# Two attentions in one launch: A's softmax reductions cut into smaller pieces in more steps, and scores ahead of maxima in the first step of the late groups

## The chip, the core and the metric

The kernel runs on one core of a Trainium2 chip. A core has a matrix engine (TensorE, PE), a vector engine (DVE), a scalar engine (ACT), a general engine (POOL) and a queue that issues DMAs (SyncE, SP). Each runs its own list of instructions in order; they meet only where one waits for another. Times are microseconds of device time, the lower the better; the time of a kernel is the median of several runs. Before the change it is 1596.72 us (three runs, 1595.77 to 1596.78).

## The reference

Two attentions with 32 heads of 18 columns over 2048 positions. A looks at 8 positions back, two apart; B at all positions. Their outputs stand side by side.

```python
def _A_ref(x, wqkv, wo):
    ...
    W, dil = 8, 2
    idx = pos[:, None] - off[None, :]
    mask = idx >= 0
    ...
    logits = jnp.einsum("bhsd,bhswd->bhsw", q, kg) * scale
    logits = jnp.where(mask[None, None, :, :], logits, -1e9)
    attn = _softmax(logits, axis=-1)
    o = jnp.einsum("bhsw,bhswd->bhsd", attn, vg)
    return (lambda x, *d: x.transpose(*d))(o, 0, 2, 1, 3).reshape(B, S, D) @ wo

def _B_ref(x, wqkv, wo):
    ...
    scores = jnp.einsum("bhqd,bhkd->bhqk", q, k) * scale
    p = _softmax(scores, axis=-1)
    o = jnp.einsum("bhqk,bhkd->bhqd", p, v)
    return (lambda x, *d: x.transpose(*d))(o, 0, 2, 1, 3).reshape(B, S, D) @ wo
a = _A_ref(A_x, A_wqkv, A_wo)
b = _B_ref(B_x, B_wqkv, B_wo)
return jnp.concatenate([a, b], axis=-1)
```

## The kernel before

The projections of both attentions come first, up to about 420 us. Then the kernel goes through 512 steps written out by hand. A step is (g, b, kt): a group g of 4 heads of B (8 groups), a block b of 512 queries (4 blocks), a piece kt of 128 keys (16 pieces). So n = step // 16 counts the pairs (g, b) that the diff calls groups behind 22, and kt = step % 16.

In a usual step the engines do this. PE makes four score matrices of 128 x 512 (`score`, line 271) and the products for the maxima of a later block (`take`, line 160): two of 512 columns, and two halves of 256 columns that share a bank (`parts_of_maximum`). Then it multiplies the exponentials of the step before with v into `po` (`weigh`, line 744, sixteen instructions that show as x8 or x16). ACT takes the exponential of the four scores (line 279). DVE reduces the three banks of maxima (`reduce`, line 168). A bank of maxima is free again once DVE has reduced it, and there are three such banks; a bank of scores is free once ACT has read it. DVE has a few other things beside them: the last reduction of a block's maxima (line 178, `m`), its transpose (line 185, `mt`), a reciprocal of B's denominators (line 788) and a copy of `po` (line 759).

What else is due in a step stands in an agenda (`plan`, `later`); `due()` issues it behind the step's own work, so on DVE a piece that is due in step s stands behind that step's three reductions and ahead of those of step s + 1.

A's attention is done beside B's steps, in eight tiles j of 256 positions (`local(j)`). Tile j begins at step AT[j] = 10, 67, 123, 178, 233, 288, 343, 398. Its parts, counted from there: `match` (steps 5 to 25, POOL) makes products of q and k, and ends with the addition that makes the logits `lg`, 128 x 8 x 64 (line 932); `most` (32 and 33, DVE, line 943) takes the maxima over the window of 8, 32 columns in a step; `lower` (33, POOL, line 949) subtracts them; `exponents` (35, ACT, line 952); `total` (36, DVE, line 943) sums over the window, 64 columns at once, or 32 in each of steps 36 and 37 for tiles 0, 2 and 5; `inverses` (38 and 39, DVE, line 959); `share` (39, POOL, line 962) multiplies the exponentials with the inverses; `weighted` (9 parts from step 39 on, POOL, lines 968 to 971) multiplies with v; `upper` and `rest` split the result (60 and 61) and `put` stores it (64 and 66). `SOON` = (3, 0, 0, 0, 1, 1, 1, 0) has these parts begin so many steps sooner (`weighted`, `upper`, `rest` and `put` are put back again by its remainder by 3). The next tile's `match` stands behind them on POOL.

`MADE` lists four steps for each tile. In the step behind each, A's sums are made: that step and the next are then done together as a pair (`together`), with the matrix products of A's output projection between the scores. A pair takes longer than two usual steps.

In the first step of a block (kt = 0) the order on PE is a choice, `ahead`: where it is true, the step's first score stands in front of the first half of a maximum, else behind it. It is true for n < 6, and for n from 24 on except in steps of `MADE`.

Of the kernel before, what the change touches and what calls it, by code (L numbers as in the profile page):

```python
# [11 lines left out]
ALU = mybir.AluOpType  # L12
# [17 lines left out]
SUB = AB // 4  # L30
# [14 lines left out]
MADE = ((96, 101, 112, 128), (144, 160, 176, 192), (208, 212, 224, 240), (256, 266, 272, 288),  # L45
        (307, 320, 336, 352), (368, 376, 384, 400), (417, 432, 440, 448), (474, 476, 478, 480))
# [4 lines left out]
def ap(t, *dims):  # L51

    return bass.AP(tensor=t.tensor, offset=t.offset, ap=[list(t.ap[0])] + [list(d) for d in dims])


def rows(t, *dims):

    return bass.AP(tensor=t.tensor, offset=t.offset, ap=[list(d) for d in dims])
# [3 lines left out]
def two_attentions(ctx: ExitStack, tc, xa, wa, woa, xb, wb, wob, out):  # L62
# [19 lines left out]
    def bank(kind=None):  # L82
        r = rings[kind or ring]
        r.append(r.pop(0))
        return p_bank.tile([128, 512], F32, name=f"bank{r[-1]}")
# [22 lines left out]
    step = 0  # L108
# [8 lines left out]
    def due():  # L117
        for f in agenda.pop(step, []):
            f()
# [89 lines left out]
    def settle():  # L209
        while owing:  # L210
            owing.popleft()()
# [171 lines left out]
    with (tc.tile_pool(name="x", bufs=1, side="right") as xp,  # L383
# [103 lines left out]
        if True:  # L487
# [47 lines left out]
            ahead = deque()  # L535
# [147 lines left out]
            for k in range(2, 14):  # L683
                n = 46 if k == 2 else 36 + 4 * k
# [7 lines left out]
            def leave_a(c, b, n, ps):  # L692
                o = xp.tile([128, 512], F32, name="ohi", bufs=4)
                nc.scalar.activation(o[:n], ps, AF.Copy)  # L694
                load(da[128 * c : 128 * c + n, HALO + 512 * b : HALO + 512 * b + 512], o[:n])
# [23 lines left out]
            for c, b in order:  # L719
                n = min(128, 3 * D - 128 * c)  # L720
                work_list.append(((b % 2, ws[c][0], xas[b][0], slice(0, n), every),
                                  lambda ps, n=n: ps[:n], lambda ps, c=c, b=b, n=n: leave_a(c, b, n, ps)))
# [12 lines left out]
        step = 0  # L735
# [166 lines left out]
    def local(j):  # L902
# [13 lines left out]
        def window(t, c):  # L916

            return ap(t[:, 2 * c, HALO:], (HALO + SUB, 2), (-DIL, W), (1, SUB))

        def wide():  # L920
            return work.tile([128, 2, W, SUB], F32, name="pr", bufs=2)
# [12 lines left out]
                    for w in range(1, W):  # L934
                        nc.gpsimd.memset(lg[:32, w, : DIL * w], MASKED)

        def over_window(op, name, n, parts=2):

            if n == 0:
                st[name] = work.tile([128, SUB], F32, name=name, bufs=1)  # L940
            some = SUB // parts
            cols = slice(some * n, some * n + some)
            nc.vector.tensor_reduce(st[name][:, cols], st["lg"][:, :, cols].rearrange("p w n -> p n w"), axis=AX.X, op=op)  # L943

        def most(n):
            over_window(ALU.max, "am", n)

        def lower():
            nc.gpsimd.tensor_sub(st["lg"], st["lg"], ap(st["am"], (0, W), (1, SUB)))
# [2 lines left out]
            nc.scalar.activation(st["lg"], st["lg"], AF.Exp, scale=SCALE)  # L952

        def total(n):
            over_window(ALU.add, "as", n, len(sums[0]))

        def inverses(n):
            half = st["as"][:, SUB // 2 * n : SUB // 2 * n + SUB // 2]
# [5 lines left out]
        def weighted(c):  # L964
            if c == 0:
                st["o"] = work.tile([128, DH, SUB], F32, name="ao", bufs=1)
            at = wide()
            nc.gpsimd.tensor_mul(at, ap(st["lg"], (0, 2), (SUB, W), (1, SUB)), window(st["v"], c))  # L968
            nc.gpsimd.tensor_add(at[:, :, :4], at[:, :, :4], at[:, :, 4:])  # L969
            nc.gpsimd.tensor_add(at[:, :, :2], at[:, :, :2], at[:, :, 2:4])  # L970
            nc.gpsimd.tensor_add(st["o"][:, 2 * c : 2 * c + 2], at[:, :, 0], at[:, :, 1])
# [10 lines left out]
        def put(i):  # L982
            load(rows(dao[j, i, 0, 0], (DH * SUB, 128), (1, DH * SUB)),
                 ap(st["parts"][i].bitcast(F32), (1, DH * SUB)))
# [24 lines left out]
        def sums_of_a(h, n, alone=True):  # L1009
# [7 lines left out]
            if not alone:  # L1017
# [4 lines left out]


        soon = SOON[j]
        sums = ((36, 37) if j in (0, 2, 5) else (36,), (38, 39))
        late = soon % 3
        pieces = [(33, lower), (35, exponents), (39, share), (60 + late, upper), (61 + late, rest), (64 + late, lambda: put(0)), (66 + late, lambda: put(1))]

        pieces[:0] = [(at, lambda f=f, n=n: f(n)) for f, ats in ((most, (32, 33)), (total, sums[0]),
                                                                (inverses, sums[1])) for n, at in enumerate(ats)]  # L1030
        for c in range(DH // 2):
            pieces.append((39 + 5 * c // 2 + late, lambda c=c: weighted(c)))
        pieces = [(at - soon, f) for at, f in pieces]
        pieces += [(5 + 5 * c // 2, lambda c=c: match(c)) for c in range(DH // 2)]

# [60 lines left out]
    sums = {}  # L1096
# [141 lines left out]
    rest = NG * NB * PIECES * 2 - early  # L1238

    total = early + rest  # L1240

    def together(both, y):

        at = [(*divmod(s // NT, NB), s % NT) for s in (step, step + 1)]
        es = [[None] * 4 for _ in range(2)]
        ps = bank("scores")[:, : y.shape[1]]
        held = rings["scores"].pop()
        exps = deque()

        def one(i, h):  # L1250
            f = score(*at[i], h, put_off=True)
            exps.append(lambda: es[i].__setitem__(h, f()))

        def others(r):
            return [f for i in range(2) for h in (r, r + 2)
                    for f in (lambda i=i, h=h: one(i, h), lambda: maximum(r)())[:: 1 - 2 * r]]

        def piece(r, k):
            a, b = both[r][k]
            return nc.tensor.matmul(ps, a, b, start=r == k == 0, stop=r == 1 and k == len(both[1]) - 1)  # L1260

        def in_turn(*lanes):

            for _, f in sorted(((at + every * k, f) for fs, at, every in lanes for k, f in enumerate(fs)), key=lambda p: p[0]):
                f()
                while len(exps) > 1:
                    exps.popleft()()

        last = []
        in_turn(([lambda k=k: last.append(piece(0, k)) for k in range(len(both[0]))], 0, 133), (others(1), 1, 235))  # L1270
        between = nc.scalar.nop()
        sync(between, last[-1])
        upper = others(0)
        if leaving:
            upper[2] = lambda f=upper[2], copy=leaving.pop(): (f(), exps.popleft()(), copy())
        in_turn(([lambda k=k: sync(piece(1, k), between) if k == 0 else piece(1, k) for k in range(len(both[1]))], 240, 133),
                (upper, 0, 235))
        while exps:
            exps.popleft()()
        nc.scalar.activation(y, ps, AF.Copy)  # L1280
        rings["scores"].append(held)
        rings["scores"].append(rings["scores"].pop(0))
        return [(*at[i], es[i]) for i in range(2)]
# [4 lines left out]
    while step < ALL:  # L1288
        n, kt = divmod(step, NT)
        g, b = divmod(n, NB)  # L1290
        es = [None] * 4

        if inside and inside[0] in for_two and kt and len(ready) == 1 and total - sum(given) >= 8 and step + 4 < ALL:
            new = together(*inside.pop(0)(False))
            assert not leaving
            due()
            step += 1
            weigh(*ready, new[0])
            ready[:] = new[1:]
            due()  # L1300
            step += 1
            continue

        while leaving:
            leaving.pop()()

        whole = total - sum(given) > 1
        parts = (bool(begun) or total - sum(given) > 3) and step not in copied

        ps = bank() if inside and whole else None  # L1310


        ahead = kt == 0 and (n < 6 or n >= 24) and step not in sum(MADE, ())
        part = [parts_of_maximum()] if parts and not ahead else []
        for h in (0, 2, 1, 3):

            if inside and h == 3:
                inside.pop(0)()
            es[h] = score(g, b, kt, h, between=(lambda: part.append(parts_of_maximum())) if parts and ahead and h == 0 else None)
            if h == 0 and whole:  # L1320
                maximum(1, ps)()
            if h == 1 and parts:
                part[0]()
            if h == 3 and whole:
                maximum(0)()
        if sum(given) == total and not begun:
            settle()
        for fs in (behind_scores, outside):
            while fs:
                fs.pop(0)()  # L1330

        paired = paired or kt % 2 == 0 and sum(given) == total and not begun
        for _ in range(1 if paired and step < ALL - 2 else len(waiting)):
            if waiting:
                waiting.pop(0)()
        if ready and (kt % 2 == 0 or not paired):
            weigh(ready.pop(0))
        ready.append((g, b, kt, es))
        if paired and kt % 2:
            weigh(*ready)  # L1340
            ready.clear()
        due()

        if len(waiting) > (0 if not paired else 2 if kt % 2 else len(waiting)):
            waiting.pop(0)()
        step += 1
# [24 lines left out]
```

## Time and profile before

| | |
|---|---|
| median of 3 runs | 1596.72 us (1595.77 to 1596.78) |
| the profiled execution | 1597.76 us, of which its span is 1596.0 us |
| granted TensorE clock | 0.999 |
| DVE's idle time in front of line 168, of it until PE's line 160 is done | 121.6 us, 91.1 us |
| POOL's idle time in front of line 962, waiting for the inverses of line 959 | 63.9 us, 6 times |
| POOL's idle time in front of line 949, waiting for the maxima of line 943 | 41.3 us, 8 times |

In a line of the timeline stand the start, the duration, the engine, the line of the kernel, the operation, what it writes and reads with the shapes, and how many alike follow each other; idle time of 150 ns or more in front of it and what ended it stand in brackets. A line of the table of groups has the number of instructions, then their busy time in all, the mean of one in ns, and the idle time in front of them. The starts of the line with `po` (744) on PE are a clock of the steps: there is one in each.

### The profile page before, as it was taken

The page shows a single profiled execution, that of the slowest core. Times are in us where ns is not written, and L with a number is a line of the kernel's source. Part 1 is how long each engine was busy: PE and PEld are TensorE (multiplying, and loading weights), DVE is VectorE, ACT ScalarE, POOL GpSimd, SP SyncE. Part 2 cuts the span into 40 slices and gives each one's busy share as a digit, 9 for nine tenths or more (in the row PEclk, how much of TensorE's full clock was granted, in tenths as well). Part 3 has the DMA queues.
Part 4 walks back from the last instruction along what each step waited for, and adds up shares of the span by engine and source line. Part 5 has one row for each costly group of instructions (what it writes and reads, how often), then busy time and mean ns, then how long its engine had stood idle before and what let it go on. Part 6 is the DMA issues. An engine that isn't in the chain of part 4 may idle for free.

```text
span 1596.0 us, 34951 instructions
## 1 busy us (share of the span) xinstructions
PE 1583.2 (99%) x13276; PEld 969.1 (61%) x13276; DVE 1367.7 (86%) x2294; ACT 1216.6 (76%) x2438; POOL 964.6 (60%) x798
## 2 busy tenths in 40 slices
PE   9999999999999999999999999999999999999998
PEld 7999889999644445444445445445444444545676
DVE  5199899999999999999989999999999999998622
ACT  6423441211599999999999999999999999998655
POOL 2405742211166996896797897797798699791000
PEclk9999999999999999999999999999999999999999
DMA  8937954622312262245326324522721332154311
GB/s 254 232 124 201 255 178 124 164 90 81 74 34 71 64 143 63 70 118 123 74 67 138 90 79 114 123 67 54 148 89 50 90 94 56 51 166 139 129 60 63
DMA packets 188024, 175.65 MB, mean 110 GB/s; under 512 B 119416, under 2 KB 133240, under 8 KB 186128
## 3 DMA queue, kind: packets, MB, share of 16 engines
q1 hardware_dynamic: 182992, 161.88, 37.0%
q0 software_dynamic: 4032, 10.63, 3.2%
q8 instruction: 104, 1.70, 0.5%
q10 hardware_dynamic: 832, 0.92, 0.2%
q14 instruction: 64, 0.52, 0.1%
HBM read 98.77 MB, written 73.47 MB: 108 GB/s over the span
## 4 chain that ended last, share of the span: by engine, by line
PE 92%; DVE 5%; DMA 1%; ACT 1%; POOL 1%; issue 0%; SPq 0%; POOLq 0%; DVEq 0%; ACTq 0%
PE po L744 29%; PE bank L271 18%; PE bank L160 17%; PE bank L366 15%; PE bank L303 5%; PE bank L1260 4%; PE bank L1133 4%; DVE mx L168 4%; POOL xlo L414 1%; ACT e L279 0%; DMA dqk<-olo 0%; DVE am L943 0%; DMA first<-xb 0%; DMA more<-xa 0%; DMA dqk<-ohi 0%
## 5 line engine op out<-in xcount | busy, mean ns | idle before, releaser
L168 DVE TENSOR_REDUCE mx<-bank 128x2 f32<-128x512 f32 x2048 | 1279.7, 684 | 121.6 <-PE bank L160 91.1
L279 ACT ACTIVATE e<-bank 128x512 f32<-128x512 f32 x2048 | 1048.3, 605 | 61.2 <-PE bank L271 55.3
L160 PE MATMUL bank<-ks,qs 54*128 54x512 f32 (+1 forms) x2466 | 789.0, 381 | 4.2 <-DVE mx L168 3.4
L160 PEld LDWEIGHTS bank<-ks,qs 54*128 54x128 f32 x2466 | 404.1, 184 | 390.2 <-DVE mx L168 343.8
L271 PE MATMUL bank<-qs,ks 56*128 56x512 f32 x2048 | 592.2, 425 | 0.1
L744 PE MATMUL po<-e,v 128*19 128x512 f32 x4096 | 531.3, 598 | 0.0
L271 PEld LDWEIGHTS bank<-qs,ks 56*128 56x128 f32 x2048 | 308.3, 184 | 25.5 <-ACT e L279 18.8
L925 POOL TENSOR_TENSOR pr<-aq,akv 128x1024 f32<-128x1024 f32 x72 | 158.4, 2201 | 15.9 <-PE po L744 13.1
L968 POOL TENSOR_TENSOR pr<-lg,akv 128x1024 f32<-128x1024 f32 x72 | 158.3, 2199 | 0.5
L744 PEld LDWEIGHTS po<-e,v 128*19 128x19 f32 x4096 | 73.8, 97 | 138.2 <-issue 132.8
L929 POOL TENSOR_TENSOR pr<-pr 128x1024 f32<-128x1024 f32 x64 | 152.5, 2383 | 5.0
L694 ACT ACTIVATE ohi<-bank 128x512 f32<-128x512 f32 (+1 forms) x56 | 30.4, 595 | 148.9 <-issue 114.0
L366 PE MATMUL bank<-xhi,ahi 64*128 64x512 f32 (+1 forms) x448 | 115.4, 387 | 0.0
L366 PE MATMUL bank<-xhi,alo 64*128 64x512 f32 (+1 forms) x448 | 111.3, 387 | 0.0
L366 PE MATMUL bank<-xlo,ahi 64*128 64x512 f32 (+1 forms) x448 | 108.3, 388 | 0.1
L1260 PE MATMUL bank<-wohi,at 64*128 64x288 f32 x480 | 104.1, 305 | 0.0
L969 POOL TENSOR_TENSOR pr<-pr 128x512 f32<-128x512 f32 x72 | 92.5, 1285 | 5.6
L1260 PEld LDWEIGHTS bank<-wohi,at 64*128 64x128 f32 x480 | 74.9, 184 | 27.6 <-ACT e L279 23.8
L414 POOL TENSOR_TENSOR alo<-raw,ahi 128x512 fp32r<-128x512 f32 (+1 forms) x14 | 17.6, 1254 | 121.1 <-ACT ahi L413 96.3
L506 POOL TENSOR_TENSOR olo<-olo,ohi 128x512 fp32r<-128x512 f32 x36 | 46.1, 1294 | 65.7 <-ACT ohi L505 55.6
L1260 PE MATMUL bank<-wolo,at 64*128 64x288 f32 x240 | 70.2, 293 | 0.0
L366 PEld LDWEIGHTS bank<-xhi,ahi 64*128 64x128 f32 (+1 forms) x448 | 65.0, 182 | 2.6
(200 smaller groups left out, 1797.3 us busy)
## 6 DMA issues: line engine op xcount, KB each, us to landing
do<-n SPq DMA_DIRECT2D x30, 512.0 KB
da<-ohi SPq DMA_DIRECT2D x52, 256.0 KB
akv<-da SPq DMA_DIRECT2D x64, 175.5 KB
out<-y SPq DMA_DIRECT2D x32, 288.0 KB
qs<-dqk SPq DMA_DIRECT2D x30, 288.0 KB
ks<-dqk SPq DMA_DIRECT2D x30, 288.0 KB
at<-dao SPq DMA_DIRECT2D x60, 128.0 KB
rec<-drec SPq DMA_DIRECT2D x29, 256.0 KB
```

Source lines behind the costliest of these rows:

```text
L160: return nc.tensor.matmul(ps if part is None else ps[:, 256 * r : 256 * r + 256], qs[at, b, p, 128 * t : 128 * t + 128], ks[at, p, 512 * k ...
L168: nc.vector.tensor_reduce(at, ps.rearrange("q (s n) -> q s n", s=2), axis=AX.X, op=ALU.max)
L271: nc.tensor.matmul(ps, ks[at, p, 128 * kt : 128 * kt + 128], qs[at, b, p], start=True, stop=True)
L279: nc.scalar.activation(e, ps, AF.Exp, scale=SCALE)
L303: nc.tensor.matmul(ps, a, b, start=c == i == 0, stop=c == 4 and i == 1)
L366: nc.tensor.matmul(ps, a, b, start=start, stop=stop)
L744: nc.tensor.matmul(po[32 * i : 32 * i + 19], vs[g][:, kt, 19 * i : 19 * i + 19], es[i], start=kt == 0, stop=kt == NT - 1)
L925: nc.gpsimd.tensor_mul(pr, ap(st["q"][:, 2 * c], (SUB, 2), (0, W), (1, SUB)), window(st["k"], c))
L929: nc.gpsimd.tensor_add(st["pr"], st["pr"], pr)
L968: nc.gpsimd.tensor_mul(at, ap(st["lg"], (0, 2), (SUB, W), (1, SUB)), window(st["v"], c))
L969: nc.gpsimd.tensor_add(at[:, :, :4], at[:, :, :4], at[:, :, 4:])
L1260: return nc.tensor.matmul(ps, a, b, start=r == k == 0, stop=r == 1 and k == len(both[1]) - 1)
```

## The change

`most` goes from two pieces of 32 columns in steps 32 and 33 to four pieces of 16 in steps 30 to 33; for tiles 3, 4 and 5 to pieces of 24, 20 and 20 in steps 31 to 33. `total` goes to four pieces of 16 in steps 36 to 39 for tiles 0, 2 and 5, and to pieces of 32, 16 and 16 in steps 36 to 38 for the others. `inverses` go from steps 38 and 39 to 39 and 40 (40 and 41 for tiles 0, 2 and 5), `share` from 39 to 40 (41), and no part of `weighted` is issued ahead of it. `lower` and `exponents` stay. `ahead` is now true for n < 6 and n >= 23 whether or not the step is in `MADE`.

```diff
-        def over_window(op, name, n, parts=2):
-            if n == 0:
+        def over_window(op, name, a, z):
+            if a == 0:
                 st[name] = work.tile([128, SUB], F32, name=name, bufs=1)
-            some = SUB // parts
-            cols = slice(some * n, some * n + some)
+            cols = slice(a, z)
             nc.vector.tensor_reduce(st[name][:, cols], st["lg"][:, :, cols].rearrange("p w n -> p n w"), axis=AX.X, op=op)
...
-            over_window(ALU.max, "am", n)
+            over_window(ALU.max, "am", *highest[n])
...
-            over_window(ALU.add, "as", n, len(sums[0]))
+            over_window(ALU.add, "as", *summed[n])
...
-        sums = ((36, 37) if j in (0, 2, 5) else (36,), (38, 39))
+        alone = j in (0, 2, 5)
+        summed = [(16 * n, 16 * n + 16) for n in range(4)] if alone else [(0, 32), (32, 48), (48, 64)]
+        highest = [(0, 24), (24, 44), (44, 64)] if j in (3, 4, 5) else [(16 * n, 16 * n + 16) for n in range(4)]
...
-        pieces = [(33, lower), (35, exponents), (39, share), ...
+        pieces = [(33, lower), (35, exponents), (40 + alone, share), ...
-        pieces[:0] = [(at, lambda f=f, n=n: f(n)) for f, ats in ((most, (32, 33)), (total, sums[0]),
-                                                                (inverses, sums[1])) for n, at in enumerate(ats)]
+        pieces[:0] = [(at, lambda f=f, n=n: f(n)) for f, ats in ((most, range(34 - len(highest), 34)),
+                                                                (total, range(36, 36 + len(summed))),
+                                                                (inverses, (39 + alone, 40 + alone))) for n, at in enumerate(ats)]
         for c in range(DH // 2):
-            pieces.append((39 + 5 * c // 2 + late, lambda c=c: weighted(c)))
+            pieces.append((max(39 + 5 * c // 2 + late, 40 + alone), lambda c=c: weighted(c)))
...
-        ahead = kt == 0 and (n < 6 or n >= 24) and step not in sum(MADE, ())
+        ahead = kt == 0 and (n < 6 or n >= 23)
```

In the built program ACT's and SP's instructions stand in the same order as before. On PE the order differs in five places, the steps 368, 384, 400, 432 and 448, where the first score and the first half of a maximum change places. DVE has 29 instructions more: 29 reductions for the maxima instead of 16, and 27 for the sums instead of 11. On POOL the order differs around four of the eight `share`: what was due in the steps that `share` has moved past now stands in front of it (a split of A's weights at tile 0, the split of a block's maxima, lines 103 and 104, at tile 4, one subtraction of line 793 at tile 5, and small ones at tile 7).

More of the change, by code (lines that the diff above doesn't have):

```diff
@@ L1024, in local @@
         soon = SOON[j]
-        sums = ((36, 37) if j in (0, 2, 5) else (36,), (38, 39))
+        alone = j in (0, 2, 5)
+        summed = [(16 * n, 16 * n + 16) for n in range(4)] if alone else [(0, 32), (32, 48), (48, 64)]
+        highest = [(0, 24), (24, 44), (44, 64)] if j in (3, 4, 5) else [(16 * n, 16 * n + 16) for n in range(4)]
         late = soon % 3
-        pieces = [(33, lower), (35, exponents), (39, share), (60 + late, upper), (61 + late, rest), (64 + late, lambda: put(0)), (66 + late, lambda: put(1))]
-        pieces[:0] = [(at, lambda f=f, n=n: f(n)) for f, ats in ((most, (32, 33)), (total, sums[0]),
-                                                                (inverses, sums[1])) for n, at in enumerate(ats)]
+        pieces = [(33, lower), (35, exponents), (40 + alone, share), (60 + late, upper), (61 + late, rest), (64 + late, lambda: put(0)), (66 + late, lambda: put(1))]
+        pieces[:0] = [(at, lambda f=f, n=n: f(n)) for f, ats in ((most, range(34 - len(highest), 34)),
+                                                                (total, range(36, 36 + len(summed))),
+                                                                (inverses, (39 + alone, 40 + alone))) for n, at in enumerate(ats)]
         for c in range(DH // 2):
-            pieces.append((39 + 5 * c // 2 + late, lambda c=c: weighted(c)))
+            pieces.append((max(39 + 5 * c // 2 + late, 40 + alone), lambda c=c: weighted(c)))
         pieces = [(at - soon, f) for at, f in pieces]
```

## The prediction

> **What bounds the kernel now.** I read the head of the page first, then the table of DVE's groups with shapes kept apart, then the timeline around A's reductions, and last POOL's part of it.
>
> ```profile
> span 1596.0 us, 34951 instructions
> PE 1583.2 (99%) x13276; PEld 969.1 (61%) x13276; DVE 1367.7 (86%) x2294; ACT 1216.6 (76%) x2438; POOL 964.6 (60%) x798
> PE 92%; DVE 5%; DMA 1%; ACT 1%; POOL 1%; issue 0%; SPq 0%; POOLq 0%; DVEq 0%; ACTq 0%
> ```
>
> The chain runs through PE, and the 5% of DVE in it are places where PE had to wait for a bank of maxima. The steps show how close DVE is to setting the pace. The starts of line 744 are the clock; the am rows are today's maxima of tile 0.
>
> ```profile
> 499.68 1.05 PE L744 MATMUL po<-e,v 128*19 128x512 f32 x8
> 501.08 0.61 DVE L943 TENSOR_REDUCE am<-lg 128x32 f32<-128x256 f32 x1
> 501.70 1.05 PE L744 MATMUL po<-e,v 128*19 128x512 f32 x8
> 503.40 0.60 DVE L943 TENSOR_REDUCE am<-lg 128x32 f32<-128x256 f32 x1
> 503.97 1.05 PE L744 MATMUL po<-e,v 128*19 128x512 f32 x8
> 506.30 1.06 PE L744 MATMUL po<-e,v 128*19 128x512 f32 x8
> ...
> 515.20 1.05 PE L744 MATMUL po<-e,v 128*19 128x512 f32 x8
> 516.63 0.34 DVE L959 RECIPROCAL as<-as 128x32 f32<-128x32 f32 x1
> 517.26 1.05 PE L744 MATMUL po<-e,v 128*19 128x512 f32 x8
> ```
>
> A step takes 2.02 us (501.70 - 499.68). Behind a maximum of 32 columns the next one takes 2.27, then 2.33: 0.25 and 0.31 lost, 0.28 in the mean above some 2.03. The step that follows a reciprocal of 0.34 us takes 2.06, so that is hidden but for 0.03. DVE can thus hide a little over 0.3 us in a step; what goes beyond is paid by the whole kernel.
>
> **The pieces.** These are the rows for DVE's work in question.
>
> ```profile
> L168 DVE TENSOR_REDUCE mx<-bank 128x2 f32<-128x512 f32 x2048 | 1279.7, 684 | 121.6 <-PE bank L160 91.1 <-PE bank L1260 3.7 <-PE bank L366 0.9
> L943 DVE TENSOR_REDUCE am<-lg 128x32 f32<-128x256 f32 x16 | 9.7, 605 | 0.0
> L178 DVE TENSOR_REDUCE m<-mx 128x16 f32<-128x128 f32 x32 | 8.9, 277 | 0.0
> L185 DVE STREAM_TRANSPOSE mt<-m 128x32 f32<-128x32 f32 x32 | 6.3, 198 | 0.0
> L959 DVE RECIPROCAL as<-as 128x32 f32<-128x32 f32 x16 | 5.4, 341 | 0.0
> L943 DVE TENSOR_REDUCE as<-lg 128x64 f32<-128x512 f32 x5 | 5.3, 1064 | 1.9 <-ACT lg L952 1.9
> ```
>
> No row has 16 columns. The line through 605 (32) and 1064 (64) rises 14.3 ns a column from 146 ns, which gives 375 ns for 16, 433 for 20, 490 for 24. Below it lies 277 (line 178 reads as many elements, 128), above it 605 (half the work at the price of the whole). I take 375: two rows of the same operation make the line, and it is nearer to the row with as many elements. At 375 a piece is just above the hidden 341: I charge 0.04 for 16 columns, 0.10 for 20, 0.16 for 24, 0.28 for 32.
>
> Maxima today: 16 x 0.28 = 4.5, less one that stands in the tail of a pair (tile 3, below): 4.2. After: twenty pieces of 16, two of them in a tail, 18 x 0.04 = 0.7; tiles 4 and 5 2 x (0.16 + 0.10 + 0.10) = 0.7; tile 3's last piece and three of 16 fall into steps that also hold an m (0.28), an mt (0.20) or a reciprocal of B's, an estimated 0.9 together, since nothing is left there to hide them. That is 2.3, **1.9 won**.
>
> Sums: tiles 0, 2 and 5 have six of 32 columns, 1.7 today, and twelve of 16 after, with two reciprocals more to the crowd, 0.7: 1.0 won. The other five have one of 64 columns today, in four of them in the tail of a pair, where DVE stands idle anyway. After, the 32 columns stay there, but two pieces of 16 and the reciprocals go into usual steps, and m or mt is in some of these too: 0.2 in each tile by the same prices, **1.0 lost**. Together 0.
>
> **The first step of a block.** What the exchange of score and maximum is worth shows at step 368, against step 416, where the score stands in front already.
>
> ```profile
> 1212.90 1.05 PE L744 MATMUL po<-e,v 128*19 128x512 f32 x8
> 1214.26 0.18 PEld L271 LDWEIGHTS bank<-qs,ks 56*128 56x128 f32 x1 [0.19 <-issue]
> 1215.27 1.05 PE L744 MATMUL po<-e,v 128*19 128x512 f32 x8
> ...
> 1319.86 1.05 PE L744 MATMUL po<-e,v 128*19 128x512 f32 x8
> 1322.02 1.05 PE L744 MATMUL po<-e,v 128*19 128x512 f32 x8
> ```
>
> Step 368 takes 2.37: the first score of a block waits for the loads of its maxima, one after another, and behind a maximum that itself waits for DVE these waits aren't done early. Step 416 takes 2.16. In the built program the score has all eight of these waits at steps 368, 400, 432 and 448, 0.2 won in each; at 384 it has two, and there 2.16 replaces a usual 2.02, 0.14 lost. That is 0.7 won, but 368 and 384 to 400 lie ahead of maxima that will wait for POOL (next part), which eats what is won before them: **0.4**.
>
> **What is moved: `share`, and with it all of POOL.** The inverses stand one step later (two in tiles 0, 2, 5), so `share` does. I asked what POOL does from a tile's `share` to the next tile's logits.
>
> ```profile
> 766.44:866.97 100.53, 100.46 (x824) 47.83 (x822) 92.41 (x153) 97.45 (x193) 96.87 (x70) 1.00 0.41 96
> ```
>
> The columns are the stretch and its length, then PE, PEld, DVE, ACT and POOL: POOL is busy 96.87 of 100.53 us with 70 instructions, 3.66 over 69 gaps, 53 ns each, which is only the distance of two instructions. No row of its timeline in this stretch has an idle bracket, except at `share` itself. POOL is full from each `share` to the next logits, so these come later by what `share` is late. Today the first maximum finds them ready:
>
> ```profile
> 766.44 1.29 POOL L962 TENSOR_TENSOR lg<-lg,as 128x512 f32<-128x512 f32 x1 [12.69 <-DVE as L959]
> 865.69 1.28 POOL L932 TENSOR_TENSOR lg<-pr 128x512 f32<-128x512 f32 x1
> 869.38 0.62 DVE L943 TENSOR_REDUCE am<-lg 128x32 f32<-128x256 f32 x1
> 983.56 1.28 POOL L932 TENSOR_TENSOR lg<-pr 128x512 f32<-128x512 f32 x1
> 988.80 0.60 DVE L943 TENSOR_REDUCE am<-lg 128x32 f32<-128x256 f32 x1
> 1105.44 1.29 POOL L932 TENSOR_TENSOR lg<-pr 128x512 f32<-128x512 f32 x1
> 1109.23 0.60 DVE L943 TENSOR_REDUCE am<-lg 128x32 f32<-128x256 f32 x1
> 1224.16 1.29 POOL L932 TENSOR_TENSOR lg<-pr 128x512 f32<-128x512 f32 x1
> 1230.82 0.60 DVE L943 TENSOR_REDUCE am<-lg 128x32 f32<-128x256 f32 x1
> 1348.28 1.28 POOL L932 TENSOR_TENSOR lg<-pr 128x512 f32<-128x512 f32 x1
> 1353.84 0.61 DVE L943 TENSOR_REDUCE am<-lg 128x32 f32<-128x256 f32 x1
> ```
>
> From the end of the logits to the first maximum these are 2.41, 3.96, 2.50, 5.37 and 4.28 us for tiles 3 to 7. The change takes from it on both sides: the first maximum comes sooner by one step (2.04) in tiles 4 and 5 and two (4.07) in 6 and 7, and the logits come later. By how much follows from the tile before, less the work that `share` now lets past itself, which POOL does while it stands idle anyway:
>
> ```profile
> L793 POOL TENSOR_TENSOR n<-o,n 128x512 fp32r<-128x512 f32 x28 | 36.0, 1284 | 1.3
> L104 POOL TENSOR_TENSOR mt<-mt,mh 128x32 fp32r<-128x32 f32 x32 | 8.1, 252 | 2.6
> L103 POOL CAST mh<-mt 128x32 fp32r<-128x32 f32 x32 | 6.7, 210 | 97.9 <-DVE mt L185 97.9
> ```
>
> Tile 4: 2.04 later, 2.04 + 2.04 - 3.96 = 0.1 us of waiting. Tile 5: 2.04 - 0.46 (lines 103, 104) = 1.58; 2.04 + 1.58 - 2.50 = 1.1. Tile 6: 4.07 - 1.28 (line 793) = 2.79; 4.07 + 2.79 - 5.37 = 1.5. Tile 7: 4.07 + 2.04 - 4.28 = 1.8.
>
> Tile 3 needs more rows, as tile 2's inverses stand in the tail of a pair today, and tile 3's first maxima in another.
>
> ```profile
> 771.11 1.89 DVE L168 TENSOR_REDUCE mx<-bank 128x2 f32<-128x512 f32 x3 [0.18 <-PE bank L160]
> ...
> 870.72 1.89 DVE L168 TENSOR_REDUCE mx<-bank 128x2 f32<-128x512 f32 x3 [0.71 <-PE bank L160]
> ```
>
> Step 164 ends on DVE at 770.93 (771.11 - 0.18); the last inverse then ends 0.34 later and `share` can start at some 771.4, 5.0 behind today's 766.44. The logits end at 866.97 + 5.0 = 871.9. Two pieces (24 and 20 columns) that are due in the pair then take 0.8, so DVE is free at 872.7 instead of 870.72, where the next reduction starts today behind 0.71 of idle time: 2.0. The work of tiles 1 and 2 I leave at no wait.
>
> A wait of DVE is paid in full: behind the first maximum stand the three reductions of the next step, PE waits for the banks that they free, and behind PE's waiting product stand the scores that feed ACT. In all 2.0 + 0.1 + 1.1 + 1.5 + 1.8 = **6.5 lost**. `weighted`, `upper` and `rest` are later with `share`, and so SP's stores of the result, with loads queued behind them. I cost that at nothing: tile 2 stores at step 189 and its first sums are made in step 209, 20 steps or some 41 us later; without that cover a pair would wait for its load.
>
> **The sum**: -1.9 + 0 - 0.4 + 6.5 = +4.2. The profiled execution (1597.76, span 1596.0) goes to 1602.0. It lies 1.04 above the median of the runs, 1596.72, which goes to **1600.9**.
>
> **The rivals.** (a) The logits aren't late: POOL makes up the time, because its spans are rough, or its instructions are shorter when DVE's stand elsewhere. For it speaks that no maximum waits today; against it the full stretch above. From the point where DVE's wait is zero in all tiles, only the gains are left: -1.9 - 0.7 = -2.6, 1594.1, not slower. 14%. (b) Half of the lateness is made up, in part by the 0.7 us that are idle at a pair's tail and the 0.2 in each step: +4.2 - 3.2, 1597.7. 15%. (c) The pieces cost nothing at all and nothing waits: -4.2 - 1.7 - 0.7 = -6.6, 1590.1; the reciprocal's row speaks for it, the crowd of m and mt against it. 7%. (d) Each of the 29 added instructions pays its fixed 146 ns on the path and nothing is won by spreading: +4.2 - 0.7 = +3.5, 1600.2, without a wait for logits. The reciprocal that is hidden speaks against it. 6%. [...]
>
> My own case has 58%.
>
> **How the numbers follow.** The time is that of my case, 1600.9. Its own range is 1598.5 to 1604: each wait may be off by 0.5. Above that lies the dearer piece: at 605 ns the 42 pieces of 16 columns would lose 10 us more (0.24 each), which the rows 605 and 1064 all but exclude, so the range goes only to 1604.5. At 277 ns they would all be hidden and win 1.7. Downwards it takes in (b) and most of (a), to 1594.5. About 0.2% (3.2 us) is what a measurement of this kernel can tell from no change. Slower by more than that: four fifths of my case and half of (d), and a little of (b), 54%. Faster: (c) and a third of (a), 12%. The rest 34%.
>
> **What would show it.** Idle time of DVE in front of line 943 (942 after) that ends with POOL's logits, 1 to 2.5 us in tiles 3, 5, 6 and 7 and none in tiles 0 to 2; POOL full from `share` to logits as today; pieces of 16 columns at 0.375 us and steps of 2.05 to 2.1 around those that don't wait; steps 368, 400, 432 and 448 at 2.16. It is wrong if the maxima wait for nothing, or if DVE's waits don't lengthen the steps.

## The result, and the profile after

| | before | changed |
|---|---|---|
| median of 6 runs each, us | 1596.75 (1595.42 to 1598.99) | 1602.62 (1602.05 to 1603.84) |
| the profiled execution, us | 1597.76 | 1602.72 |
| ratio of the medians | | 1.0037 (95%: 1.0024 to 1.005) |

The kernel is 5.87 us slower (1602.62 - 1596.75), where the prediction has 1600.9, 4.2 slower. The head of the page of the changed kernel comes first.

```profile
span 1600.9 us, 34982 instructions
PE 1582.5 (99%) x13276; PEld 960.2 (60%) x13276; DVE 1367.2 (85%) x2323; ACT 1217.0 (76%) x2438; POOL 965.8 (60%) x798
PE 75%; POOL 14%; DVE 4%; DMA 3%; issue 2%; ACT 1%; SPq 1%; POOLq 0%; DVEq 0%
```

The busy times have hardly moved: DVE has 29 instructions more and 0.5 us less to do, POOL 1.2 us more. What has moved is the chain: POOL had 1% of it and has 14%. The chain is followed backwards and runs along POOL from a tile's logits to its `share` and on, so it says where something waits for POOL, and not that 14% of the time was lost there. The view of the waits gives the size. Its columns are the sum in us, the number and the longest.

```profile
DVE am L942 <- POOL lg L932: 7.5, 4, 2.5
PE bank L160 <- DVE mx L168: 8.2, 8, 2.0
```

The first row has no counterpart before: the maxima never waited for the logits. The second reads so in the kernel before:

```profile
PE bank L160 <- DVE mx L168: 3.4, 15, 0.4
```

There were 15 pieces of at most 0.4 us; now there are single pieces of 2.0. DVE waits for POOL, and PE, which gets no bank back in the meantime, for DVE. The timeline shows the four places and, in its first line, the late `share` of tile 2.

```profile
769.22 1.28 POOL L961 TENSOR_TENSOR lg<-lg,as 128x512 f32<-128x512 f32 x1 [17.42 <-DVE as L958]
...
868.46 1.28 POOL L932 TENSOR_TENSOR lg<-pr 128x512 f32<-128x512 f32 x1
869.78 0.81 DVE L942 TENSOR_REDUCE am<-lg 128x24 f32<-128x192 f32 x2 [2.47 <-POOL lg L932]
...
1107.34 1.29 POOL L932 TENSOR_TENSOR lg<-pr 128x512 f32<-128x512 f32 x1
1108.66 0.49 DVE L942 TENSOR_REDUCE am<-lg 128x24 f32<-128x192 f32 x1 [1.27 <-POOL lg L932]
...
1228.13 1.28 POOL L932 TENSOR_TENSOR lg<-pr 128x512 f32<-128x512 f32 x1
1229.45 0.37 DVE L942 TENSOR_REDUCE am<-lg 128x16 f32<-128x128 f32 x1 [1.79 <-POOL lg L932]
...
1354.09 1.28 POOL L932 TENSOR_TENSOR lg<-pr 128x512 f32<-128x512 f32 x1
1355.40 0.37 DVE L942 TENSOR_REDUCE am<-lg 128x16 f32<-128x128 f32 x1 [1.93 <-POOL lg L932]
```

In tiles 3, 5, 6 and 7 the first maximum starts just as the logits end, behind 2.47, 1.27, 1.79 and 1.93 us of idle time. `share` of tile 2 starts 2.78 us later than before in absolute time (769.22 against 766.44); but the changed kernel's steps are some 2.1 us ahead of the old ones by then, so against the steps it is 4.9 later, where the prediction has 5.0. Between `share` of tile 2 and the logits of tile 3 POOL is as full as before. The columns of the next view are the stretch and its length, then PE, PEld, DVE, ACT and POOL.

```profile
769.22:869.75 100.53, 100.45 (x827) 47.83 (x825) 90.83 (x151) 96.96 (x193) 96.88 (x70) 1.00 0.37 87
```

It is the same 100.53 us, with the same 70 instructions and 96.88 us of work (96.87 before). In none of the seven stretches from a `share` to the next logits does POOL's timeline have an idle bracket, before or after. What `share` is late, the logits are late.

The pieces themselves are in the table of DVE's groups.

```profile
L942 DVE TENSOR_REDUCE as<-lg 128x16 f32<-128x128 f32 x22 | 8.1, 371 | 0.0
L942 DVE TENSOR_REDUCE am<-lg 128x16 f32<-128x128 f32 x20 | 7.4, 372 | 3.7 <-POOL lg L932 3.7
...
L942 DVE TENSOR_REDUCE am<-lg 128x20 f32<-128x160 f32 x6 | 2.6, 432 | 0.0
L942 DVE TENSOR_REDUCE am<-lg 128x24 f32<-128x192 f32 x3 | 1.5, 492 | 3.8 <-POOL lg L932 3.7
```

The prediction's line through 32 and 64 columns gave 375, 433 and 490 ns; they take 372, 432 and 492. And step 368, which took 2.37 us, is now 2.15 (1215.92 - 1213.77), where 2.16 was predicted:

```profile
1213.77 1.05 PE L744 MATMUL po<-e,v 128*19 128x512 f32 x8
1215.92 1.05 PE L744 MATMUL po<-e,v 128*19 128x512 f32 x8
```

To see where the 5.87 us come from, I took the start of each step's first exponential (line 279) as a clock and subtracted the one kernel's from the other's, counted from step 1 on. Up to there, in the projections, the changed kernel's profiled execution was 0.87 us ahead (more on that in the last section), so its own 4.96 us (1602.72 - 1597.76) are 5.82 lost in the steps. The lag grows and shrinks in these places:

| place | predicted | measured |
|---|---|---|
| tile 3, maxima wait | +2.0 | +1.92 |
| tile 5, maxima wait | +1.1 | +1.53 |
| tile 6, maxima wait | +1.5 | +2.07 |
| tile 7, maxima wait | +1.8 | +2.04 |
| behind tile 6's wait, TensorE at half its clock | not in the sum | +1.21 (0.69 and 0.52 in two steps) |
| all the rest: pieces, sums, exchange, tile 4 | -2.2 (-1.9 - 0.4 + 0.1) | -2.95 (what is left of 5.82) |
| sum | +4.2 | +5.82 |

The fifth row is the one that the prediction doesn't have. After tile 6's wait PE looks like this in the timeline:

```profile
1228.03 1.05 PE L744 MATMUL po<-e,v 128*19 128x512 f32 x8
1231.07 0.38 PE L160 MATMUL bank<-ks,qs 54*128 54x256 f32 x1 [1.99 <-DVE mx L168]
...
1232.11 1.49 PE L744 MATMUL po<-e,v 128*19 128x512 f32 x8
```

The same eight products take 1.05 us ahead of the idle time and 1.49 behind it. The windows have the granted clock in the third column from the end:

```profile
1229.00:1232.00 3.00, 1.01 (x12) 0.71 (x8) 2.55 (x7) 0.98 (x3) 2.85 (x4) 1.00 0.02 5
1232.00:1236.00 4.00, 4.00 (x22) 1.65 (x24) 3.50 (x8) 3.32 (x8) 1.08 (x3) 0.57 0.00 0
1236.00:1238.00 2.00, 2.00 (x20) 0.85 (x16) 1.47 (x4) 1.28 (x3) 1.18 (x1) 1.00 0.00 0
```

From 1232.6 to 1236.0 the granted clock is 0.50; ahead of it PE was busy for 1.01 of 3 us.

### The profile page after: what moved, and what is told of

The parts are those of the page before. It is cut to its first block, busy times and chain, and to the rows that moved or that the text cites. A ratio compares the mean times of both kernels' runs of the same rounds, so it can differ in the third digit from the quotient of the medians.

```text
span 1600.9 us, 34982 instructions
## 1 busy us (share of the span) xinstructions
PE 1582.5 (99%) x13276; PEld 960.2 (60%) x13276; DVE 1367.2 (85%) x2323; ACT 1217.0 (76%) x2438; POOL 965.8 (60%) x798
## 4 chain that ended last, share of the span: by engine, by line
PE 75%; POOL 14%; DVE 4%; DMA 3%; issue 2%; ACT 1%; SPq 1%; POOLq 0%; DVEq 0%
PE po L744 21%; PE bank L366 15%; PE bank L271 13%; PE bank L160 13%; PE bank L303 5%; PE bank L1135 4%; DVE mx L168 3%; POOL pr L925 3%; PE bank L1262 3%; POOL pr L929 3%; POOL pr L967 2%; POOL pr L968 1%; DMA ks<-dqk 1%; ACT e L279 1%; POOL pr L969 1%
## 5 line engine op out<-in xcount | busy, mean ns | idle before, releaser
L103 POOL CAST mh<-mt 128x32 fp32r<-128x32 f32 x32 | 6.8, 212 | 115.3 <-DVE mt L185 115.3
```

## The experiments

The theory: `share` is issued later, POOL is full from there to the next logits, and the sooner maxima meet later logits on DVE; everything else wins a little. The main rivals: the 29 small reductions cost the time themselves, each by its fixed part; or the wait is only a matter of the maxima standing too early, whatever `share` does.

**The exchange alone.** Before, with the new `ahead`:

```diff
-        ahead = kt == 0 and (n < 6 or n >= 24) and step not in sum(MADE, ())
+        ahead = kt == 0 and (n < 6 or n >= 23)
```

> The kernel before with the exchange of score and maximum alone (steps 368, 384, 400, 432, 448). Theory (late logits are what costs; the exchange wins): four of the five steps some 0.25 us shorter, 384 0.1 longer, no wait of DVE for POOL: 0.9 us faster, about 1595.8. Rival (the exchange itself is what made the changed kernel slower, since it delays DVE's first bank in five blocks): slower by 1 to 5 us, 1598 to 1602.

Measured: 1595.95 against 1596.16, ratio 0.9998 (0.9988 to 1.0007): no difference that runs can tell, where 0.9 us were expected. The step clock can: the lag changes by -0.25 in step 368, -0.25 in 400 and -0.27 in 448, by +0.11 in 384, and in tile 7 by -0.43 and then +0.36. So a score in front wins 0.25 us in a step, loses 0.1 in step 384, and of the sum of -0.7 only -0.3 is left at the end.

**The maxima undone.** The changed kernel with two pieces of 32 columns:

```diff
-        highest = [(0, 24), (24, 44), (44, 64)] if j in (3, 4, 5) else [(16 * n, 16 * n + 16) for n in range(4)]
+        highest = [(0, 32), (32, 64)]
```

> The changed kernel with the maxima as before (two pieces of 32 columns in steps 32 and 33); sums, inverses, share and the exchange as changed. Theory: share is as late as in the changed kernel, but the first maximum no longer comes sooner, so the logits are late in tile 3 only (5.0 us later against 2.4 in hand): one wait of DVE of about 2.6 us, of which 0.7 falls into the idle tail of a pair, 1.9 lost; sums 0, exchange 0.9 won: 1.0 us slower than before, 1597.7. Rival (the added instructions cost, not the waits): 16 of the 29 are still there, so more than half of the 5.9 us stays, 1600.

Measured: 1597.52, ratio 1.0008 (0.9998 to 1.0018). In the waits one of the four is left, tile 3's:

```profile
DVE am L942 <- POOL lg L932: 2.5, 1, 2.5
```

It costs 1.68 us in the step clock. With the maxima back where they were, tiles 5 to 7 have room for the late logits.

**The sums undone, and `share` with them.** The changed kernel with the sums, inverses, `share` and `weighted` of before; maxima and exchange stay as changed:

```diff
-        summed = [(16 * n, 16 * n + 16) for n in range(4)] if alone else [(0, 32), (32, 48), (48, 64)]
+        summed = [(0, 32), (32, 64)] if alone else [(0, 64)]
...
-        pieces = [(33, lower), (35, exponents), (40 + alone, share), ...
+        pieces = [(33, lower), (35, exponents), (39, share), ...
-                                                                (inverses, (39 + alone, 40 + alone))) for n, at in enumerate(ats)]
+                                                                (inverses, (38, 39))) for n, at in enumerate(ats)]
-            pieces.append((max(39 + 5 * c // 2 + late, 40 + alone), lambda c=c: weighted(c)))
+            pieces.append((39 + 5 * c // 2 + late, lambda c=c: weighted(c)))
```

> The changed kernel with sums, inverses and share in the steps and pieces of before; maxima in small pieces from step 30 or 31 and the exchange as changed. Theory: share is on time, so POOL's logits are ready before the sooner maxima in every tile (in hand today 2.4 to 5.4 us, used up 0 to 4.1): no wait of DVE for POOL, 1.9 us won by the pieces and 0.9 by the exchange: 2.8 us faster than before, 1593.9. Rival (added instructions): 13 of the 29 are there at 0.15 us each, 1.9 us slower less the exchange's 0.9: 1597.7. Rival (the earlier maxima alone are what makes DVE wait): waits of about 2 us in tiles 6 and 7 stay, 1597 to 1598.

Measured: 1594.54 against 1596.16, ratio 0.9989 (0.9979 to 0.9998). No maximum waits, so the sooner maxima alone are not what makes DVE wait. The steps end 2.52 us ahead, the medians lie 1.6 apart; 2.8 were expected. With 13 of the 29 added reductions still in it the kernel is faster than before; that speaks against a price of each small instruction. Its timeline gives the room that the sooner maxima leave:

```profile
865.16 1.29 POOL L932 TENSOR_TENSOR lg<-pr 128x512 f32<-128x512 f32 x1
868.87 0.84 DVE L942 TENSOR_REDUCE am<-lg 128x24 f32<-128x192 f32 x2
...
1223.34 1.29 POOL L932 TENSOR_TENSOR lg<-pr 128x512 f32<-128x512 f32 x1
1225.70 0.38 DVE L942 TENSOR_REDUCE am<-lg 128x16 f32<-128x128 f32 x1
```

From the end of the logits to the first maximum there are 2.42 us in tile 3 (868.87 - 866.45) and 1.07 in tile 6; read in the same way, 1.85 in tile 4, 0.43 in tile 5 and 0.06 in tile 7. Take from these what the prediction says the logits are late (some 5.0, 2.04, 1.58, 2.79 and 2.04 for tiles 3 to 7): -2.6, -0.2, -1.15, -1.7, -2.0. The changed kernel's waits are 2.47, 0.10 (too short for a bracket), 1.27, 1.79 and 1.93.

**`share` late, nothing else.** Before, with the inverses, `share` and `weighted` at the changed steps, whole sums and maxima:

```diff
-        pieces = [(33, lower), (35, exponents), (39, share), ...
+        pieces = [(33, lower), (35, exponents), (40 + alone, share), ...
-        sums = ((36, 37) if j in (0, 2, 5) else (36,), (38, 39))
+        alone = j in (0, 2, 5)
+        sums = ((36, 37) if alone else (36,), (39 + alone, 40 + alone))
...
-            pieces.append((39 + 5 * c // 2 + late, lambda c=c: weighted(c)))
+            pieces.append((max(39 + 5 * c // 2 + late, 40 + alone), lambda c=c: weighted(c)))
```

> The kernel before with nothing but the inverses one step later (two in tiles 0, 2 and 5) and share with them; the reductions whole and in their old steps, no exchange. No instruction is added. Theory: POOL's logits are later by as much, and in tile 3 later than the maximum: one wait of DVE for POOL of about 2.6 us, 1.9 lost: 1598.6; lg of each tile 2 to 5 us later against the step of its first maximum. Rival (POOL catches up, the changed kernel's waits come from the earlier maxima alone): no wait, 1596.7.

Measured: 1598.4 against 1596.16, ratio 1.0016 (1.0006 to 1.0025).

```profile
DVE am L943 <- POOL lg L932: 2.5, 1, 2.5
```

Without any small piece the same wait stands in tile 3 and costs 1.64 us in step 212. So, in the steps, `share` alone costs 1.6, maxima and exchange alone win 2.5, which would add up to -0.9; the whole change costs 5.8. The 6.7 between are, in the table above, the waits of tiles 5 to 7 (1.53 + 2.07 + 2.04 = 5.64) and the half clock (1.21): they need both the late `share` and the sooner maxima.

**`share` kept, the rest taken.** The third experiment's kernel with tile 7's sum in two pieces and step 384 taken out of `ahead`:

```diff
+        summed = [(0, 32), (32, 64)] if alone or j == 7 else [(0, 64)]
...
+        ahead = kt == 0 and (n < 6 or n >= 23) and step != 384
```

> A version meant to beat both: maxima in small pieces as changed; inverses and share in the steps of before; sums as before, but in two pieces of 32 in tile 7, where the one of 64 lies in front of a usual step; the exchange in steps 368, 400, 432 and 448, not in 384. Theory: no wait of DVE for POOL; the 2.5 us of the version with the sums undone, 0.1 for step 384 and some 0.4 for tile 7: 3.0 us faster than before, 1593.2. Rival (small pieces don't pay beyond measurement): 1594.5 to 1596.

Measured: 1594.61 against 1596.58, ratio 0.9987 (0.9978 to 0.9996): faster than both kernels, by 2.0 and by 8.0 us. But it misses the number expected of it by 1.4, lies in the range of its rival, and is no better than the third experiment. Tile 7's two pieces won 0.45 us in step 436 and gave 0.47 back in step 437.

```profile
span 1592.3 us, 34965 instructions
PE 94%; DVE 3%; POOL 1%; ACT 1%; issue 0%; DMA 0%; SPq 0%; POOLq 0%; DVEq 0%
```

The chain is back to POOL's 1%, and DVE's share falls from 5% to 3%.

**The maxima of tiles 6 and 7 one step later.** The changed kernel with three pieces there too:

```diff
-        highest = [(0, 24), (24, 44), (44, 64)] if j in (3, 4, 5) else [(16 * n, 16 * n + 16) for n in range(4)]
+        highest = [(0, 24), (24, 44), (44, 64)] if j in (3, 4, 5, 6, 7) else [(16 * n, 16 * n + 16) for n in range(4)]
```

> The changed kernel with the three pieces (24, 20, 20 from step 31) in tiles 6 and 7 too, so their first maximum comes one step later; all else as changed. Theory: the waits of DVE in tiles 6 and 7 shrink by a step of 2.04 us each, from about 1.8 and 2.0 to nothing or 0.2; the other two waits (tiles 3 and 5) stay; with tile 6's wait the stretch of half clock behind it goes. 1602.6 less 4.0 and less 1.2, plus 0.4 for the larger pieces: 1597.8. Rival (the waits come from the lateness alone, whatever the step of the maxima): 1602.

Measured: 1597.69, ratio 1.0005 (0.9996 to 1.0014).

```profile
DVE am L942 <- POOL lg L932: 3.6, 2, 2.4
```

One step of 2.04 us is more than the 1.79 and 1.93 of waiting; both waits are gone, the half clock behind them too (the execution's granted clock of 0.999 leaves room for one stretch of 3.4 us, and it has one at 175 us, where the windows read down to 0.58), and tiles 3 and 5 keep theirs. That is 4.9 us less than the changed kernel, for two waits that cost 4.1 and a half clock of 1.2, less what the dearer pieces take.

**The changed kernel twice more,** unedited, for the half clock:

> The changed kernel once more, for its trace: the four waits of DVE for POOL's logits are the same to 0.1 us; open is whether TensorE's half-speed stretch of 3.4 us behind tile 6's wait comes again (theory: PE's idle time of 2 us there brings it, so it does, or one behind another of the waits) or not (rival: it falls anywhere, as the one at 175 us of the kernel before).

> The changed kernel a third time, for its trace, with the same question: where the stretch of half clock falls.

Measured: 1602.41 and 1602.65, one execution each. The four waits come again, though each is 0.1 to 0.2 us shorter (6.9 and 7.0 us in all, against 7.5). The half clock isn't the same: the first has it behind tiles 6 and 7, from 1230.7 and 1357.0 on (0.50 in the 3.40 us from each), the second only behind tile 7. There the windows read

```profile
1352.00:1355.00 3.00, 1.72 (x15) 0.48 (x11) 1.18 (x4) 2.19 (x5) 2.92 (x4) 1.00 0.16 63
1355.80:1359.20 3.40, 3.40 (x18) 1.28 (x18) 2.77 (x6) 2.06 (x4) 2.74 (x3) 0.50 0.22 73
1360.00:1362.00 2.00, 2.00 (x18) 0.82 (x16) 2.00 (x5) 1.94 (x5) 0.01 (x1) 1.00 0.30 104
```

So in these three executions it isn't tied to a tile. What a stretch costs shows against the same two steps of an execution that has none there. Behind tile 6 (steps 375 and 376) the lag grows by 1.21 and 1.28 with the stretch and by -0.05 without it; behind tile 7 (431 and 432) by 0.96 and 0.81 with it and by -0.51 without it. That is 1.3 to 1.5 us for each. All three profiled executions of the changed kernel have at least one.

**Less work on POOL.** The theory stands on POOL being full, so POOL was relieved without touching DVE or `share`: of the eight additions in `match` the one for the fifth pair of columns is left out (these columns then don't enter the logits), 2.4 us in each tile.

```diff
-            else:
+            elif c != 4:
                 nc.gpsimd.tensor_add(st["pr"], st["pr"], pr)
```

> The changed kernel without one of the eight additions that gather the products of q and k in each tile (the one of the fifth pair of columns is left out, 2.4 us on POOL between share and the next logits); nothing is moved. Theory (POOL is full from share to the logits, and its throughput sets how late they are): the logits come 2.4 us sooner in every tile, the four waits of DVE (today 1.2 to 2.5 us) go to nothing or 0.1, and with them the stretches of half clock behind them: 7.4 + 1.2 less, 1594 to 1594.5, as fast as the version with share on time. Rival (what delays the logits is something POOL waits for, a load or a step of the agenda): waits and time as in the changed kernel, 1602.5.

Measured, with the edit in the changed kernel: 1594.19 against 1596.63, ratio 0.9986 (0.9977 to 0.9996). The timeline at tiles 3 and 6:

```profile
865.30 1.28 POOL L932 TENSOR_TENSOR lg<-pr 128x512 f32<-128x512 f32 x1
866.69 0.83 DVE L942 TENSOR_REDUCE am<-lg 128x24 f32<-128x192 f32 x2
...
1221.75 1.28 POOL L932 TENSOR_TENSOR lg<-pr 128x512 f32<-128x512 f32 x1
1223.78 0.38 DVE L942 TENSOR_REDUCE am<-lg 128x16 f32<-128x128 f32 x1
```

No idle bracket stands in front of the maxima. All 29 added instructions are there, in the same steps, and 8.4 us are gone against the changed kernel (1602.62). The same edit in the kernel before shows what the shorter work on POOL is worth by itself:

> The kernel before without the same addition. Theory: POOL's work costs nothing there, since the logits have 2.4 us and more in hand: 1596.6, no change. [...]

Measured: 1597.14 against 1596.63, ratio 1.0005 (0.9995 to 1.0014). POOL's work as such costs nothing there; it costs 8.4 us only where DVE waits for it.

## Why the prediction was right, and where its sum was short

**The direction and the mechanism held.** The late `share`, the full POOL, the waits on DVE in tiles 3, 5, 6 and 7 and none in 0 to 2 are all in the profile; the experiment with a late `share` alone shows that `share` makes the first of them, the one with less work on POOL that relieving POOL removes all four. Rival (a), that POOL makes up the time, falls with the stretch of 100.53 us, which is as long as before; (b), half of it made up, with the four waits of 7.5 us, which lengthen the steps by 7.56; (c), in which nothing waits, with the same waits.

**Rival (d)** had 1600.2, not far from the forecast, from a fixed price of each small instruction. The number alone could not tell it from the forecast; the waits can, and the experiments. With the sums undone 13 of the 29 added reductions are left, with less work on POOL all 29, and both times the kernel is 1.6 to 2.4 us faster than before as long as nothing waits. The fixed part is there (372 ns for half of what takes 601); but a usual step has room for nearly all of a piece of 372 ns and not for one of 601: behind tile 0's four maxima of 16 columns the changed kernel's steps take 2.02, 2.08, 2.09 and 2.09 us, behind its two of 32 columns those of before 2.27 and 2.33, and the usual ones around them 2.02 to 2.05.

**The waits were mis-sized by 1.2** (7.56 against 6.4 in these four tiles). Tile 3 was right, 1.92 for 2.0. In tiles 6 and 7 the prediction left the gain of steps 368 and 384 to 400 out, since the waits would eat it. They do, but by becoming longer: the kernel with the sums undone has 1.07 and 0.06 us of room where the prediction's distances leave 1.30 and 0.21 (5.37 - 4.07 and 4.28 - 4.07). That is the same gain booked in another place and changes no sum; it makes the rest larger (next point). A second part: in tiles 5 to 7 the steps lose 0.26, 0.28 and 0.11 more than DVE waits. Most of that is no matter of waiting, since the same steps lose 0.17, 0.20 and 0.04 in the kernel with less work on POOL, where nothing waits. It is the price of the small pieces there, which the prediction has in another term; less than 0.1 in each tile is left for the wait beyond its own length.

**The gains were right where nothing waits.** The prediction adds them up for that case in its rival (a): -1.9 - 0.7 = -2.6. In the step clock the kernel with the sums undone ends 2.52 us ahead, and the one with less work on POOL, which has the sums in pieces, 2.40. So the pieces of the sums are worth nothing or cost 0.1, where the prediction has 0. The 2.95 of the table are more than the 2.2 of the prediction mostly because the rows above hold whole steps: in the same six steps these two kernels lose 0.34 and 0.36 without any wait, and outside of them they win 2.86 and 2.76.

**The term that was missing is the half clock,** +1.21. The step that fell short is "A wait of DVE is paid in full", taken as the whole price: the wait is paid, and behind that of tile 6, which left PE idle for 1.99 us, a second price followed, because PE then ran at half its clock for 3.4 us (0.50 from 1232.6 to 1236.0). The sum of 4.2 was short by 1.6: in the table's rows 1.2 in the waits and 1.2 for the clock, less 0.75 in the rest. Set against the kernel with less work on POOL, in which nothing waits, the waits and the half clock cost 8.2 us in the steps (5.82 + 2.40). The prediction has 6.8 for them, 6.5 and the 0.3 of gain that they eat; most of what is missing is the half clock. How near the forecast came is in part luck: the three profiled executions of the changed kernel had one, two and one such stretches, and their steps lost 5.8, 6.9 and 5.7 us.

## What to carry to other kernels

Where an in-order engine is full from one hand-over to the next, as POOL was here with 96.87 of 100.53 us, moving its first piece by one step moves everything behind it, and the price appears a whole tile later, at another line (`share` of tile 2 was 4.9 us later against the steps, and the maxima of tile 3 waited 2.47); measure the distance between hand-over and use there before moving either end. Two moves that are harmless or useful alone (+1.6 and -2.5 us here) can eat the same distance from both sides (+5.8 together), so each goes in by itself. Small pieces are worth their fixed cost where each step has idle time that hides one but not the larger one, as the steps here did with 372 and 601 ns.

## What was not expected of the hardware

The granted clock of TensorE fell to 0.50 for 3.4 us behind some idle times of PE of 1.7 us and more, and not behind others of the same length. In the first profiled execution of the changed kernel it fell behind the 1.99 us of tile 6 and stayed whole (1.00 in the 3.40 us behind each) behind the 1.85 us of tile 3, the 1.41 of tile 5 and the 1.96 of tile 7. The windows of tiles 6 and 7:

```profile
1232.60:1236.00 3.40, 3.40 (x20) 1.51 (x16) 2.90 (x6) 2.72 (x7) 0.48 (x3) 0.50 0.00 0
1357.00:1360.40 3.40, 3.37 (x28) 1.68 (x32) 3.40 (x7) 2.82 (x6) 3.03 (x3) 1.00 0.16 55
```

In the two other executions, where the longest idle time of PE behind DVE is 1.8 and 1.9 us, it fell behind tiles 6 and 7 and behind tile 7: four times out of nine for tiles 3, 6 and 7 in all three. What sets apart the idle times behind which it fell was not shown. Their length alone does not: 1.96 us passed without it here, and 1.70 in the kernel before (below) didn't. No run set the length or the place of one.

This also bears on the 0.87 us ahead of step 1. In the projections PE waits once for ACT at some 174 us, as the timeline of the kernel before shows, and its windows have the half clock behind it:

```profile
175.16 0.59 PE L366 MATMUL bank<-xhi,whi 64*128 64x512 f32 x2 [1.70 <-ACT olo L504]
```

```profile
175.40:178.80 3.40, 3.40 (x18) 2.64 (x18) 1.41 (x3) 3.29 (x7) 3.32 (x3) 0.50 0.94 323
```

In the changed kernel's execution the idle time was even longer, and the clock stayed whole:

```profile
175.89 0.50 PE L366 MATMUL bank<-xhi,whi 64*128 64x512 f32 x2 [1.95 <-ACT olo L504]
```

```profile
175.40:178.80 3.40, 2.91 (x26) 2.40 (x28) 2.10 (x4) 3.29 (x6) 3.30 (x5) 1.00 0.93 268
```

The code is the same there in all twelve executions. The idle time was 0.62 to 2.23 us in them; behind the eight of 1.70 us or more the clock fell five times, behind the four shorter ones never. At step 1 the five with the half clock lie between 0.00 and 0.65 us behind the kernel before's execution, which is one of them, and the seven without it 0.78 to 2.22 ahead. So executions differ there by up to 2.9 us though their code is the same, in part by the half clock, and the step clock was therefore counted from step 1.
